# Gated attention over 2048 tokens on one core: sums of tokens resident in SBUF in place of a ring, loads and stores at other places of each unit

## The chip, the cores and the metric

The kernel runs on one core of a Trainium2 chip. The core has five engines, each with its own list of instructions that it works off in order: PE (matrix products), DVE (vector work), ACT (activations and copies), POOL (vector work, slower) and SP, which here only issues transfers between HBM and SBUF. The engines wait for one another by semaphores. The metric is the device time of one execution in microseconds (us); lower is better. Three runs of the kernel before took 2256.18, 2256.52 and 2259.43 us, a median of 2256.52. The profiled execution, from which every view of the trace comes, took 2265.28 us, with a span of 2263.50 on the core.

## The reference

```python
x = A_x                                   # 1 x 2048 x 640
xn = _layernorm(x, axis=-1)
q = (xn @ wq) -> 32 heads of 128
k, v = the last 512 keys of the cache, per head
scores = einsum("bhqd,bhkd->bhqk", q, k) * 128 ** -0.5
o = einsum("bhqk,bhkd->bhqd", softmax(scores), v)
s = o (all heads side by side: 4096) @ wo # 2048 x 640
h = relu(xn @ w1 + b1) ** 2               # 1728 wide
g = silu(h @ w2 + b2)
return x + s * g
```

Everything is float32.

## The kernel before, in words

**Products.** A float32 product is made of three matmuls on pairs: each operand is split into a high and a low part (`hi`, `lo`; ACT copies the high part, POOL or DVE subtracts it from the whole), and high by high, high by low and low by high are summed in PSUM. One such triple on a 128 x 128 weight and 512 tokens is three matmuls (`triple`).

**Tiling.** The tokens are four tiles of 512 (`NT`). The kernel starts with the layer norm, most of the gate (the MLP) and its spill to HBM; then come 128 *units*, one for each pair of a head and a tile. Units 0 to 63 (the first half) do tiles 0 and 3, units 64 to 127 tiles 1 and 2. Four units are a group (`UPG`): two heads by two tiles. At the end follow the rest of the MLP for tile 3 (`late_load`, `late_prep`, `late_up`: raw weights `l1r` and `l2r`, split ones `l1w` and `l2w`, products `lu` and `ly`) and the finish, which multiplies the attention sum `acc` by g (`fg`, loaded by `load_finish`) on DVE and adds x (`fx`) on POOL or DVE.

**One unit i.** PE makes the scores (`s_mm`, four PSUM banks, 12 matmuls). DVE reduces them to column maxima (`max_fold`), ACT gathers these, DVE folds them to a row (`row(i, "m")`, tile `rowm`), and SP writes the 2 KB row to HBM (`m_d`) and reads it back broadcast over the 128 partitions (`bm`, 256 KB). DVE subtracts it from the scores (`shift`, tile `e`), which frees the four score banks: the scores of unit i+1 wait for that. ACT takes exponentials (`expo`) and the high part (`p_hi`), POOL the low part (`p_lo`, tiles `pt`) and the sum of the two halves of the exponentials (`s_add`, tile `su`). DVE folds that sum (`s_fold`, tile `rds`), then `row(i, "s")` makes reciprocals, SP writes them (`s_d`) and reads them back broadcast (`bs`). During the next unit PE multiplies by the values (`v_mm`, bank `o`), DVE scales by `bs` (`o_norm`), ACT and DVE split (`ot`), and after every second unit of a tile PE applies wo (`r_mm`) and DVE adds to `acc` (`r_acc`). So in each unit two small round trips through HBM stand on SP's queue, among the loads of raw keys, values and weights (`kr`, `vr`, `or`, `qr`).

**The queries.** In the first half q comes from five triples per unit. In the second half, two heads by two tiles are done with seven products in place of eight on four of the five chunks: for this the first half makes sums of blocks of wq (`q_sums`, `q_sum_hi`, `q_sum_lo`, tiles `sw`, `ss`) and stores them split in HBM (`q_store`, `wq_d`), and the second half loads them back (`q_piece`, tile `qp`, 512 or 640 KB, one in each unit). The sums of tokens t1 to t4, each of two chunks, lie in HBM (`TS_d`). Part of them is loaded once into `XT`; six pieces of 512 KB that have no room there come anew in every group through a ring of three buffers (`q_ring`, `tr_t`: five pieces; `tr_rest`: two transfers of 256 KB for the last chunk of tile 2).

**What sets the order.** All unit work is put on a list with a time, `at(when, f, ...)`, where a unit has `PERIOD` 12.4; the list is sorted by that time and then emitted, and each engine keeps that order. The numbers are places in an order, not times on the chip. A load is thus issued by SP when SP has come to its place and its buffer is free; whatever stands behind it on SP waits too. BEHIND is a second list: transfers that `row` issues between the write and the broadcast read.

**Where code lies.** The scores of each unit start at a set place of PE's instruction memory: `align` pads to it.

```python
BLOCK, FIRST_SLOT, SLOTS = 256, 188, (0, 11, 22, 33, 42)
pe.addr_align(BLOCK, (FIRST_SLOT + BLOCK // 2 * i + slot) % BLOCK)
```

A unit has 128 slots; its first part with the scores ends at slot 42, and each other matmul takes two with its weight load, so that 54 matmuls in all fit before the next unit's first slot. A unit with more is padded up to that slot one block further on.

**Engines' shares.** Over the span PE is busy 90%, DVE 73%, POOL 60% and ACT 56%.

## Time and profile before

| What | Value |
|---|---|
| median of three runs | 2256.52 us (2256.18 to 2259.43) |
| the profiled execution | 2265.28 us |
| its span | 2263.50 us |
| mean granted clock of PE | 0.961 |
| busy PE / DVE / POOL / ACT | 2032.1 / 1662.1 / 1358.7 / 1257.9 us |
| start of unit 0 / 10 / 59 / 72 / 124 | 298.82 / 433.70 / 1124.30 / 1317.21 / 2063.92 us |
| moved over HBM | 368.69 MB, 163 GB/s |

The stretches between these starts are what the prediction's first view shows. In the views, a row of waits names the engine and its instruction, then what it waited for, the total, the number of times and the longest. A row of the timeline gives start, length, engine, operation and tiles, and in square brackets the idle time of the engine ahead of it with what ended it; `x4` is four instructions shown as one row. SPq is SP's issue of a transfer: its length is that of the issue, not of the transfer. Row names put out before in: `e<-s,bm` writes e and reads s and bm. All instructions have the line of one helper (L77), so tiles tell them apart.

### The profile page before, as it was taken

Reading aid. Unit: us, or ns where it says so; the run is one execution under the profiler, and the core shown is the slowest. Engines: PE = TensorE matmul, PEld = TensorE weight load, DVE = VectorE, ACT = ScalarE, POOL = GpSimd, SP = SyncE. Lnnn points to the kernel's source line nnn. Section 1 sums busy time; section 2 is a strip of 40 time slices with the busy share of each in tenths; the row PEclk is TensorE's granted clock in tenths of the full one; section 3 lists DMA queues with packets and bytes.
Section 4 is the critical chain, followed back from the end, with each engine's and each line's share of the span. In section 5 each row is a group of like instructions: output and inputs, shape, how many; then the busy total and the mean of one; then the engine's idle time right before and its main releaser. Section 6 shows DMA issues by size and latency. Waiting matters only on the chain. (4 is left out here: it accounts for less than half of the span.)

```text
span 2263.5 us, 29971 instructions
## 1 busy us (share of the span) xinstructions
PE 2032.1 (90%) x8489; PEld 1623.0 (72%) x8489; DVE 1662.1 (73%) x2856; ACT 1257.9 (56%) x2232; POOL 1358.7 (60%) x772
## 2 busy tenths in 40 slices
PE   9999999999999999999998888888889888988677
PEld 7887877777777777777776677666677677776566
DVE  6864557788888888888877677777777777777543
ACT  5664446655656555555555555555555555555322
POOL 1031057777777777777776566666666666667431
PEclk9999999999999999999999999999999999999888
DMA  6588744444344344434366555565555455556264
GB/s 196 173 292 293 277 149 138 133 124 122 122 121 122 122 122 122 122 122 122 121 214 205 180 171 169 177 182 179 174 167 169 167 160 165 167 166 190 69 189 143
DMA packets 214385, 368.69 MB, mean 163 GB/s; under 512 B 30084, under 2 KB 89238, under 8 KB 212950
## 3 DMA queue, kind: packets, MB, share of 16 engines
q1 hardware_dynamic: 210358, 350.63, 49.7%
q0 software_dynamic: 3728, 15.99, 1.8%
q8 instruction: 78, 1.28, 0.2%
q14 instruction: 77, 0.63, 0.1%
q10 hardware_dynamic: 144, 0.16, 0.0%
HBM read 293.81 MB, written 72.89 MB: 162 GB/s over the span
## 5 line engine op out<-in xcount | busy, mean ns | idle before, releaser
L77 POOL TENSOR_TENSOR pt<-e,pt 128x1024 fp32r<-128x1024 f32 x256 | 614.2, 2399 | 342.1 <-ACT pt L77 318.9
L77 PE MATMUL s<-q,wk 128*128 128x512 f32 x1536 | 423.9, 430 | 160.2 <-DVE e L77 144.9
L77 PE MATMUL r<-ot,wo 128*128 128x512 f32 x1920 | 494.6, 391 | 5.6 <-DVE acc L77 3.2
L77 PEld LDWEIGHTS s<-q,wk 128*128 128x128 f32 x1536 | 313.7, 208 | 257.7 <-issue 105.5
L77 ACT ACTIVATE e<-e 128x1024 f32<-128x1024 f32 x256 | 269.3, 1052 | 361.4 <-DVE e L77 345.0
L77 PEld LDWEIGHTS r<-ot,wo 128*128 128x128 f32 x1920 | 362.5, 189 | 85.0 <-DVE acc L77 5.2
L77 PE MATMUL o<-pt,wv 128*128 128x512 f32 x1536 | 389.9, 399 | 30.8 <-DVE ot L77 27.8
L77 PEld LDWEIGHTS o<-pt,wv 128*128 128x128 f32 x1536 | 285.6, 190 | 117.1 <-DVE ot L77 40.1
L77 DVE TENSOR_TENSOR e<-s,bm 128x512 f32<-128x512 f32 x512 | 315.9, 676 | 62.5 <-DMA bm<-m_d 62.0
L77 DVE TRANSPOSE_TENSOR_REDUCE rdm<-s 128x16 f32<-128x512 f32 x512 | 328.6, 686 | 38.7 <-PE s L77 38.0
L77 POOL TENSOR_TENSOR su<-e,e 128x1024 f32<-128x1024 f32 x128 | 308.1, 2407 | 0.0
L77 ACT ACTIVATE pt<-e 128x1024 fp32r<-128x1024 f32 x256 | 271.7, 1061 | 7.0
L77 PE MATMUL pq<-ax,wq 128*128 128x512 f32 x960 | 228.2, 389 | 0.0
L77 DVE TENSOR_TENSOR acc<-r,acc 128x512 f32<-128x512 f32 x300 | 200.3, 668 | 10.1 <-PE r L77 9.8
L77 PEld LDWEIGHTS pq<-ax,wq 128*128 128x128 f32 x960 | 180.2, 188 | 37.7
L77 ACT ACTIVATE rdm<-rdm 32x64 f32<-32x64 f32 x384 | 97.8, 255 | 158.7 <-DVE rdm L77 155.7
L77 DVE TRANSPOSE_TENSOR_REDUCE rds<-su 128x32 f32<-128x1024 f32 x128 | 158.3, 1237 | 2.1 <-POOL su L77 2.0
L77 POOL TENSOR_TENSOR wo<-or,wo 128x640 fp32r<-128x640 f32 x64 | 107.3, 1676 | 81.8 <-ACT wo L77 81.8
L77 ACT ACTIVATE rds<-rds 32x32 f32<-32x32 f32 x384 | 90.0, 234 | 115.3 <-DVE rds L77 111.1
L77 DVE TENSOR_TENSOR ot<-o,ot 128x512 fp32r<-128x512 f32 x128 | 88.5, 691 | 77.1 <-ACT ot L77 75.8
L77 ACT ACTIVATE ot<-o 128x512 fp32r<-128x512 f32 x128 | 76.5, 598 | 105.2 <-DVE o L77 105.1
L77 DVE TENSOR_TENSOR o<-o,bs 128x512 f32<-128x512 f32 x128 | 87.5, 684 | 63.9 <-DMA bs<-s_d 63.9
(484 smaller groups left out, 2543.4 us busy)
## 6 DMA issues: line engine op xcount, KB each, us to landing
tr_t<-ts_d SPq DMA_DIRECT2D x80, 512.0 KB
bm<-m_d SPq DMA_DIRECT2D x128, 256.0 KB
bs<-s_d SPq DMA_DIRECT2D x128, 256.0 KB
or<-in_wo_dram SPq DMA_DIRECT2D x64, 320.0 KB
qp<-wq_d SPq DMA_DIRECT2D x32, 640.0 KB
kr<-in_kT_dram SPq DMA_DIRECT2D x64, 256.0 KB
vr<-in_v_dram SPq DMA_DIRECT2D x64, 256.0 KB
wq_d<-ss SPq DMA_DIRECT2D x64, 256.0 KB
```

The costliest lines, as they stand in the source:

```text
L77: ins = method(*args, **kwargs)
```

## The change

- **The ring is gone.** Its six sums get homes in two resident tiles, `ta` and `tb` (`T_HOME`, `open_t`, `load_t`). Three are loaded in the first half, three around the turn of the halves, once. The chunk of `XT` that held a sum now holds the last chunk of tile 2, so that the rest needs no ring either.
- **Room for it.** `s_add` writes over the first half of the exponentials, without `su`. `bm` and the fold tiles have one buffer in place of two. The raw values share the raw keys' buffer, g shares x's; the order of the early finish loads is s, g, x.
- **Stores of `wq_d`** stood at one place of a unit, behind `bs` (11.9). They now stand at two, behind `bm` (4.4, `BM`) and behind `bs` (11.9, `BS`).
- **Loads of `XT` for the second half** went in lots ahead of or behind the broadcast reads in three units for each tile. They now come two transfers of 256 KB at a place, over `BM` and `BS` of units 59 to 64, and BEHIND is gone.
- **The end.** Late in the program the tiles of the sums are closed and a pool `fin` opens, where x and g have two buffers. The wo products of the last but one pair of units have places of their own (`R_AT_LAST`), one of them moved from unit 126 to unit 127. Of the late loads, `LOAD[2]` stands one place later and the first `load_late_x` one place earlier, behind `bm`.

SP's list has 1248 rows where it had 1354. PE, ACT, POOL and DVE have as many instructions of work as before, and in ACT's and POOL's order nothing moves.

SP in the second half, before: from the end of one unit through the next. The numbers in the names are counters; `tr_t` are pieces of the ring.

```order
L77 DMA bs_16816<-s_d_16814 128x512
L77 DMA or_19_16828<-in_wo_dram 128x640
L77 DMA kr_19_16830<-in_kT_dram 128x512
L77 DMA tr_t_16832<-ts_d_81 128x1024
L77 DMA m_d_16906<-rowm_16904 32x16
L77 DMA bm_16908<-m_d_16906 128x512
L77 DMA qp_2_16912<-wq_d_2_121 128x1280
L77 DMA tr_t_16932<-ts_d_81 128x1024
L77 DMA tr_t_16934<-ts_d_82 128x1024
L77 DMA s_d_16961<-rows_16957 16x32
L77 DMA bs_16963<-s_d_16961 128x512
L77 DMA vr_18_16976<-in_v_dram 128x512
```

The same stretch now:

```order
L77 DMA bs_16608<-s_d_16606 128x512
L77 DMA or_19_16620<-in_wo_dram 128x640
L77 DMA kr_19_16622<-in_kT_dram 128x512
L77 DMA m_d_16695<-rowm_16693 32x16
L77 DMA bm_16697<-m_d_16695 128x512
L77 DMA qp_2_16701<-wq_d_2_121 128x1280
L77 DMA s_d_16746<-rows_16742 16x32
L77 DMA bs_16748<-s_d_16746 128x512
L77 DMA vr_18_16761<-in_v_dram 128x512
```

Only the three `tr_t` are gone: one ahead of the write of the maxima, two between the broadcast read `bm` and the write of the sums `s_d`.

SP in the first half, the stores of the block sums, before:

```order
L77 DMA vr_24_9691<-in_v_dram 128x512
L77 DMA or_24_9693<-in_wo_dram 128x640
L77 DMA wq_d_0_131<-wq_9381 256x1x256
L77 DMA wq_d_1_132<-wq_9381 256x1x384
L77 DMA m_d_9763<-rowm_9761 32x16
L77 DMA bm_9765<-m_d_9763 128x512
```

and now, one group earlier in the program:

```order
L77 DMA vr_22_9094<-in_v_dram 128x512
L77 DMA or_22_9096<-in_wo_dram 128x640
L77 DMA m_d_9163<-rowm_9161 32x16
L77 DMA bm_9165<-m_d_9163 128x512
L77 DMA wq_d_0_127<-wq_8785 256x1x256
L77 DMA wq_d_3_130<-wq_8927 256x1x128
L77 DMA wq_d_0_127<-ss_9051 256x1x256
L77 DMA s_d_9218<-rows_9214 16x32
```

The stores moved from ahead of the write `m_d` to behind the broadcast read `bm`, ahead of `s_d`.

PE in unit 126, between its `lu` and the scores of unit 127, before, with the first of the twelve `o` that stand between `r_1` and `r_2`:

```order
L77 MATMUL r_1_20664<-ot_20362,wo_28_0_19845 128x512 x2
L77 MATMUL r_1_20664<-ot_20362,wo_28_1_19846 128x512
L77 MATMUL r_1_20664<-ot_20505,wo_29_0_19702 128x512 x2
L77 MATMUL r_1_20664<-ot_20505,wo_29_1_19703 128x512
L77 MATMUL o_20688<-pt_0_0_20593,wv_31_0_20535 128x512
```

and now the same place, and then the piece of r that follows the scores of unit 127 (`ISA` ends an aligned part):

```order
L77 MATMUL r_1_20346<-ot_20045,wo_28_0_19541 128x512 x2
L77 MATMUL r_1_20346<-ot_20045,wo_28_1_19542 128x512
L77 MATMUL o_20366<-pt_0_0_20274,wv_31_0_20218 128x512
```

```order
L77 MATMUL s_3_20421<-q_0_20204,wk_31_1_19943 128x512
L77 ISA
L77 MATMUL r_1_20346<-ot_20188,wo_29_0_19402 128x512 x2
L77 MATMUL r_1_20346<-ot_20188,wo_29_1_19403 128x512
```

Three matmuls of r went from unit 126, which held 57, to unit 127, behind its scores.

The core of the diff:

```diff
             src = TS_d[0][:, c - NQ2, i, :] if c in (2, 3) else xT_d[T1][i][:, c, :]
         elif c == DC - 1:
-            src = TS_d[3][:, 1, i, :]
+            src = xT_d[T2][i][:, c, :]
         else:
...
     def raw_tile(kind, name):
+        if "fin" in pools and kind in "vsxgw":
+            n = D if kind == "w" else W
+            return pools["fin"].tile(
+                [P, n], F32, tag=f"fin{kind}", name=name, bufs=1 if kind in "vw" else 2
+            )
         n = D if kind in "qo" else W
-        pool_of = pools["ep"] if kind in "qk" else ap
+        pool_of = pools["ep"] if kind in "qkv" else ap
+        kind = {"v": "k", "g": "x"}.get(kind, kind)
         return pool_of.tile([P, n], F32, tag=f"raw{kind}", name=name, bufs=2 if kind == "q" else 1)
 
     def pair(tag, shape, name, bufs):
...
-    def q_ring(n, what):
-        r = QR[n, what] = pools["tr"].tile(
-            [P, 2, NT], F32R, tag="tr", name=f"tr{n}_{what}", bufs=3
-        )
-        if what == "rest":
-            for i in range(2):
-                sp.dma_start(raw(r)[:, i, :], xT_d[T2][i][:, DC - 1, :])
-        else:
-            sp.dma_start(raw(r), TS_d[int(what[1]) - 1][:, int(what[2])])
+    def open_t(n):
+        QR[n] = pools["tr" + n].tile([P, 3, 2, NT], F32R, tag="t" + n, name="t" + n, bufs=1)
+
+    T_HOME = {"t20": "a0", "t21": "a1", "t30": "a2", "t31": "b0", "t40": "b1", "t41": "b2"}
+
+    def load_t(what):
+        n, j = T_HOME[what]
+        sp.dma_start(raw(QR[n])[:, int(j)], TS_d[int(what[1]) - 1][:, int(what[2])])
...
-        for args in BEHIND.pop((i, what), ()):
-            load_x2(*args)
-        bc = ap.tile([P, NT], F32, tag=f"b{what}", name=f"b{what}{i}", bufs=2 if what == "m" else 1)
+        bc = ap.tile([P, NT], F32, tag=f"b{what}", name=f"b{what}{i}", bufs=1)
...
     def s_add(i):
-        RD[i, "su"] = ap.tile([P, 2, NT], F32, tag="su", name=f"su{i}", bufs=1)
-        pool.tensor_tensor(RD[i, "su"], E[i, 0], E[i, 1], op=ALU.add)
+        RD[i, "su"] = E[i, 0]
+        pool.tensor_tensor(E[i, 0], E[i, 0], E[i, 1], op=ALU.add)
...
     def turn_over():
-        pre.close()
-        pools["tr"] = ctx.enter_context(tc.tile_pool(name="tr", bufs=1))
-
+        trb.close()
+        pools["trb"] = trb.enter_context(tc.tile_pool(name="trb", bufs=1))
+        open_t("b")
+
+    def turn_end():
+        trb.close()
+        tra.close()
+        pools["fin"] = ctx.enter_context(tc.tile_pool(name="fin", bufs=1))
+
+    BM, BS = 4.4, 11.9
...
+        for k, lo, what, *places in (
+            (0, 2, (0, 0, 2), (0, BM), (0, BM), (-2, BM)),
+            (3, 0, (0, 4, 5), (0, BM), (-1, BM), (-2, BM)),
+            (1, 0, (0, 2, 5), (0, BS), (-1, BM), (-2, BM)),
+            (2, 0, (1, 2, 5), (1, BM), (1, BM), (-1, BM)),
+            (3, 1, (1, 4, 5), (1, BM), (0, BM), (-1, BM)),
+            (0, 0, "s1", (2, BM), (0, BM), (0, BM)),
+            (1, 3, "s2", (2, BM), (1, BM), (0, BM)),
+            (2, 3, "s3", (2, BS), (2, BM), (1, BM)),
+            (3, 2, "s4", (2, BS), (2, BS), (1, BM)),
         ):
-            pre_at(u, 4.4 if end and u == 1 else 11.9, q_store, k, lo, what)
-    at((NU // 2 - 3) * PERIOD + 10.0, turn_over)
-
+            u, when = places[0 if first else 2 if end else 1]
+            pre_at(u, when, q_store, k, lo, what)
...
+    b = NU // 2
+    at((b - 24) * PERIOD, open_t, "a")
+    at((b - 3) * PERIOD + 8.0, turn_over)
...
+    for u, when, pieces in (
+        (-22, BM, ("t20",)),
+        (-18, BM, ("t21",)),
+        (-14, BM, ("t30",)),
+        (-5, BM, ((0, 2),)),
+        (-5, BS, ((0, 3),)),
+        (-4, BM, ((0, 0),)),
+        (-4, BS, ((0, 1),)),
+        (-3, BS, ((1, 0), (0, 4))),
+        (-2, BM, ((1, 1),)),
+        (-2, BS, ("t31",)),
+        (-1, BM, ("t40",)),
+        (-1, BS, ("t41",)),
+        (0, BM, ((1, 2),)),
+        (0, BS, ((1, 3), (1, 4))),
+    ):
+        for what in pieces:
+            if isinstance(what, str):
+                at((b + u) * PERIOD + when + 0.05, load_t, what)
+            else:
+                for i in range(2):
+                    at((b + u) * PERIOD + when + 0.05, load_x2, what[0], i, what[1])
...
+    R_AT_LAST = (
+        ((3 * PERIOD + 2.75, range(G)),),
+        ((3 * PERIOD + 7.75, range(1)), (4 * PERIOD + 2.75, range(1, G))),
+        ((3 * PERIOD + 11.25, range(G)),),
+        ((4 * PERIOD + 7.0, range(G)),),
+        ((4 * PERIOD + 7.6, range(G)),),
+    )
+    R_BANK_LAST = ("x", "x", 0, "x", 0)
...
-            if slot == 0:
-                on(4.45, q_ring, n, "t20")
-                on(4.45, q_ring, n, "t21")
-                on(10.4, q_ring, n, "t30")
-            elif slot == 1:
-                on(7.6, q_ring, n, "t31")
-                on(7.6, q_ring, n, "t40")
-            elif slot == 2:
-                on(4.45, q_ring, n, "rest")
...
-        2: z - 2 * PERIOD + 10.3,
+        2: z - PERIOD + 4.5,
...
-        at(z - 3 * PERIOD + (10.3, 16.8, 16.85, 22.7, 22.75)[c], load_late_x, c)
+        at(z - 3 * PERIOD + (4.5, 16.8, 16.85, 22.7, 22.75)[c], load_late_x, c)
+    at(z - 3 * PERIOD + 9.2, turn_end)
```

More of the change, by code (lines that the diff above doesn't have):

```diff
@@ L858, in bank @@
         return pools["psa"].tile([P, NT], F32, tag=f"qr{k}", name=name, bufs=1)
-    BEHIND = {}
     def open_xT(hf, t):
@@ L997, in q_right @@
     def q_right(n, what, q):
-        if (n, f"{what}{q}") in QR:
-            r = QR[n, f"{what}{q}"]
-            return r[:, 0, :], r[:, 1, :]
-        t, c = (1, 3) if what == "t4" else RES[what]
+        if f"{what}{q}" in T_HOME:
+            k, j = T_HOME[f"{what}{q}"]
+            return [QR[k][:, int(j), i, :] for i in range(2)]
+        t, c = RES[what]
         return [x[:, c + q, :] for x in XT[1, t]]
@@ L1017, in q_rest @@
         w = QP[n, k]
-        if t == 0:
-            xs = [x[:, DC - 1, :] for x in XT[1, 0]]
-        else:
-            r = QR[n, "rest"]
-            xs = r[:, 0, :], r[:, 1, :]
+        xs = [x[:, DC - 1, :] for x in XT[1, t]]
         triple(
@@ L1071, in fold_tile @@
         n = KC if what == "m" else 2
-        return ap.tile([P, NQ, P // B32, n], F32, tag=f"rd{what}", name=f"rd{what}{i}", bufs=2)
+        return ap.tile([P, NQ, P // B32, n], F32, tag=f"rd{what}", name=f"rd{what}{i}", bufs=1)
     def max_fold(i, c):
@@ L1233, in late_load @@
         else:
-            tag, bufs = ("su", 1) if kind == 1 else ("e", 2)
-            r = ap.tile([P, 2, NT], F32, tag=tag, name=f"l{kind}r{f}", bufs=bufs)
-            r = r.rearrange("p a b -> p (a b)")[:, :D]
+            if kind == 1:
+                r = raw_tile("w", f"l{kind}r{f}")
+            else:
+                r = ap.tile([P, 2, NT], F32, tag="e", name=f"l{kind}r{f}", bufs=2)
+                r = r.rearrange("p a b -> p (a b)")[:, :D]
         if kind == 1:
@@ L1323, in late_relu @@
         ph = LPH[f]
-        r = LR[f] = raw_tile(kind, f"lr{f}")[:n, :]
+        if kind == "s":
+            r = pools["tra"].tile([P, 3, 2, NT], F32, tag="ta", name=f"lr{f}", bufs=1)[:, 0, 0]
+        else:
+            r = raw_tile(kind, f"lr{f}")
+        r = LR[f] = r[:n, :]
         bias = b1_sb[:n, f : f + 1]
@@ L1395, in late_gate @@
         tag = ("bm", "bs")[(d + lo * 2 // NT) % 2]
-        sg = ap.tile([P, NT], F32, tag=tag, name=f"lsg{d}_{lo}", bufs=2 if tag == "bm" else 1)[:, : hi - lo]
+        sg = ap.tile([P, NT], F32, tag=tag, name=f"lsg{d}_{lo}", bufs=1)[:, : hi - lo]
         act.activation(sg, LPY[py], AF.Silu, bias=b2_sb[:, d : d + 1])
@@ L1552 @@
     at(10.0, pad, pools["ep"], 480)
-    pools["pre"] = pre = ExitStack()
-    pools["pre"] = pre.enter_context(tc.tile_pool(name="pre", bufs=1))
+    tra, trb = ExitStack(), ExitStack()
+    pools["tra"] = tra.enter_context(tc.tile_pool(name="tra", bufs=1))
+    pools["pre"] = trb.enter_context(tc.tile_pool(name="pre", bufs=1))
     def turn_over():
-        pre.close()
-        pools["tr"] = ctx.enter_context(tc.tile_pool(name="tr", bufs=1))
+        trb.close()
+        pools["trb"] = trb.enter_context(tc.tile_pool(name="trb", bufs=1))
+        open_t("b")
@@ L1560 @@
+    def turn_end():
[3 more added lines that the diff above has]
+    BM, BS = 4.4, 11.9
     for n in range(NG):
         base = UPG * PERIOD * n
-        end = n == NG - 1
+        first, end = n == 0, n == NG - 1
         def pre_at(u, when, f, *a):
-            at(max(base + u * PERIOD, 0.0) + when if n else max(u, 0) * PERIOD + when, f, n, *a)
-        pre_at(-2, 9.5, q_sums, 0)
-        pre_at(-1, 5.0 if end else 9.5, q_sums, 1)
+            assert n or u >= 0
+            at(base + u * PERIOD + when, f, n, *a)
+        pre_at(0 if first else -2, 9.5, q_sums, 0)
+        pre_at(0 if first else -1, 5.0 if end else 9.5, q_sums, 1)
@@ L1569 @@
         for k in range(4):
-            u = k // 2 - 1 if end else k - 1
-            if n == 0:
-                u = 1 + k // 2
+            u = 1 + k // 2 if first else k // 2 - 1 if end else k - 1
             pre_at(u, 7.0 + 0.01 * k, q_sum_hi, k)
             pre_at(u, 9.0 + 0.01 * k, q_sum_lo, k)
-        late = n == 0
-        for u, k, lo, what in (
-            (-1 + late, 0, 2, (0, 0, 2)),
-            (-1 + late, 1, 0, (0, 2, 5)),
-            (0 + late, 2, 0, (1, 2, 5)),
-            (0, 3, 0, (0, 4, 5)),
-            (0, 3, 1, (1, 4, 5)),
-            (0 if end else 1, 0, 0, "s1"),
-            (0 if end else 1, 1, 3, "s2"),
-            (1 if end else 2, 2, 3, "s3"),
-            (1 if end else 2, 3, 2, "s4"),
-        ):
-            pre_at(u, 4.4 if end and u == 1 else 11.9, q_store, k, lo, what)
@@ L1588 @@
-    at((NU // 2 - 3) * PERIOD + 10.0, turn_over)
-    for t in range(TPH):
-        u = NG * UPG + t * G - 5
-        at(u * PERIOD + 4.3, open_xT, 1, t)
-        pieces = [
-            (t, i, c) for c in ((2, 3, 0, 1, 4), (0, 1, 2, 3, 4))[t] for i in range(2)
-        ]
-        places = [(u, "bm", 1 - t), (u - 1, "s", 2 - t), (u + 1, "m", 1), (u + 1, "bm", 1)]
-        places += [(u, "s", 2), (u + 2, "m", 1), (u + 2, "bm", 1 + t), (u + 1, "s", 1 + t)]
-        for k, what, n in places:
-            for args in pieces[:n]:
-                if what == "bm":
-                    at(k * PERIOD + 4.3, load_x2, *args)
-                else:
-                    BEHIND.setdefault((k, what), []).append(args)
-            pieces = pieces[n:]
-        assert not pieces
+        for k, lo, what, *places in (
[8 more added lines that the diff above has]
+            (3, 2, "s4", (2, BS), (2, BS), (1, BM)),
+        ):
+            u, when = places[0 if first else 2 if end else 1]
+            pre_at(u, when, q_store, k, lo, what)
@@ new lines @@
+    b = NU // 2
+    at((b - 24) * PERIOD, open_t, "a")
+    at((b - 3) * PERIOD + 8.0, turn_over)
+    for t in range(TPH):
+        at((b - 5 + t * G) * PERIOD + 4.3, open_xT, 1, t)
+    for u, when, pieces in (
[17 more added lines that the diff above has]
+                at((b + u) * PERIOD + when + 0.05, load_t, what)
+            else:
+                for i in range(2):
+                    at((b + u) * PERIOD + when + 0.05, load_x2, what[0], i, what[1])
@@ L1718 @@
                         k = k[d]
+                    elif i == NU - 2 * G - 1:
+                        places, k = R_AT_LAST, R_BANK_LAST[d]
                     else:
                         places, k = R_AT_Q[t], "x"
+                        if d == 0 and i == NQS - 1:
+                            places = (
+                                ((2 * PERIOD + 11.25, range(1)), (3 * PERIOD + 2.75, range(1, G))),
+                            )
                     for when, js in places[d]:
@@ L1726 @@
                     w = (NU // 2 + 9 + 4 * d) * PERIOD
-                    for k, n in enumerate("sxg" if t == 0 else ""):
-                        at(w + k * PERIOD - 0.6, load_finish, n, 0, t, d)
                     if t == 0:
-                        at(w + 3 * PERIOD - 0.7, finish_gate, 0, t, d)
+                        for k, n in enumerate("sgx"):
+                            at(w + k * PERIOD - 0.6, load_finish, n, 0, t, d)
+                        at(w + 2 * PERIOD - 0.7, finish_gate, 0, t, d)
                         at(w + 3 * PERIOD - 0.7, finish, 0, t, d)
```

## The prediction

> **What bounds the kernel now.** I read the busy time by stage first. The cuts lie where units 10, 59, 72 and 124 start; the columns are the stretch, its length, then busy time and count of PE, PEld, DVE, ACT and POOL, the granted clock, the DMA share and GB/s.

> ```profile
> 433.70:1124.30 690.60, 632.58 (x2648) 505.31 (x2646) 560.20 (x956) 407.12 (x735) 526.77 (x296) 0.97 0.41 122
> 1124.30:1317.21 192.91, 166.02 (x681) 130.16 (x682) 137.95 (x238) 109.28 (x197) 123.43 (x63) 0.97 0.60 196
> 1317.21:2063.92 746.71, 660.71 (x2730) 522.75 (x2731) 577.38 (x994) 418.18 (x741) 488.21 (x239) 0.97 0.55 170
> 2063.92:2263.50 199.58, 154.97 (x617) 122.67 (x617) 98.53 (x151) 71.12 (x117) 74.52 (x43) 0.88 0.45 143
> ```

> No engine is full anywhere. The third stretch is 13 groups of four units, 57.44 us each, with PE busy 50.8 of it (matmuls at the slower clock included) and DVE 44.4. Next the waits of that stretch (us in total, times, longest):

> ```profile
> DVE o L77 <- DMA bs<-s_d: 40.6, 26, 2.8
> DVE e L77 <- DMA bm<-m_d: 35.3, 27, 3.1
> ```

> 26 and 27 times in 13 groups: two units of each four have DVE stand for both broadcasts, 75.9 us or 5.84 a group. PE's timeline of one group shows which units:

> ```profile
> 1751.01 2.88 PE L77 MATMUL s<-q,wk 128*128 128x512 f32 x12
> 1763.41 2.88 PE L77 MATMUL s<-q,wk 128*128 128x512 f32 x12
> 1779.98 2.97 PE L77 MATMUL s<-q,wk 128*128 128x512 f32 x12 [3.50 <-DVE e L77]
> 1794.76 2.98 PE L77 MATMUL s<-q,wk 128*128 128x512 f32 x12 [1.56 <-DVE e L77]
> 1807.45 2.88 PE L77 MATMUL s<-q,wk 128*128 128x512 f32 x12
> ```

> The units 102 to 105 take 12.40, 16.57, 14.78 and 12.69 us, 56.44 together. The two long ones end in PE waiting for e, the shift that frees the score banks. SP's issues around them say why, and two rows of the page's issue list give the sizes:

> ```profile
> 1761.86 0.32 SPq L77 DMA_DIRECT2D s_d<-rows  x1
> 1766.87 0.32 SPq L77 DMA_DIRECT2D bs<-s_d  x1
> ...
> 1768.84 0.33 SPq L77 DMA_DIRECT2D m_d<-rowm  x1
> 1774.21 0.32 SPq L77 DMA_DIRECT2D bm<-m_d  x1
> 1774.62 0.38 SPq L77 DMA_DIRECT2D qp<-wq_d  x1
> 1775.06 0.90 SPq L77 DMA_DIRECT2D tr_t<-ts_d  x2
> 1776.60 0.32 SPq L77 DMA_DIRECT2D s_d<-rows  x1
> 1783.38 0.32 SPq L77 DMA_DIRECT2D bs<-s_d  x1
> ```

> ```profile
> 1800.12 0.32 SPq L77 DMA_DIRECT2D m_d<-rowm  x1
> 1801.44 0.32 SPq L77 DMA_DIRECT2D bm<-m_d  x1
> 1801.85 0.54 SPq L77 DMA_DIRECT2D qp<-wq_d  x1
> 1806.28 0.32 SPq L77 DMA_DIRECT2D s_d<-rows  x1
> 1807.61 0.33 SPq L77 DMA_DIRECT2D bs<-s_d  x1
> ```

> ```profile
> tr_t<-ts_d SPq DMA_DIRECT2D x80, 512.0 KB
> qp<-wq_d SPq DMA_DIRECT2D x32, 640.0 KB
> ```

> The write of 2 KB and the broadcast read behind it take 1.33 us of SP where qp was issued 4.43 us before and nothing else, and 5.01 and 6.78 us where ring pieces were issued before; for the maxima 1.32 against 5.37. So the tuned bound is a queue: small round trips behind ring pieces.

> **Part A, the ring goes (units 72 to 123).** The PE, ACT, POOL and DVE instructions stay the same in number (8489 matmuls before and now). SP loses 80 ring pieces and 32 rests. Each was an issue of about 0.45 us (0.90 for two at 1775.06) on an engine that bounds nothing, so the issues count as nought; what counts is the queue. I follow the two long units on DVE and POOL:

> ```profile
> 1771.31 0.70 DVE L77 TENSOR_TENSOR o<-o,bs 128x512 f32<-128x512 f32 x1 [1.90 <-DMA bs<-s_d]
> 1773.28 1.24 DVE L77 TRANSPOSE_TENSOR_REDUCE rds<-su 128x32 f32<-128x1024 f32 x1
> 1779.14 2.48 DVE L77 TENSOR_TENSOR e<-s,bm 128x512 f32<-128x512 f32 x4 [1.99 <-DMA bm<-m_d]
> 1785.15 2.41 POOL L77 TENSOR_TENSOR su<-e,e 128x1024 f32<-128x1024 f32 x1
> 1787.48 0.70 DVE L77 TENSOR_TENSOR o<-o,bs 128x512 f32<-128x512 f32 x1 [2.18 <-DMA bs<-s_d]
> 1789.45 1.24 DVE L77 TRANSPOSE_TENSOR_REDUCE rds<-su 128x32 f32<-128x1024 f32 x1
> 1793.94 2.47 DVE L77 TENSOR_TENSOR e<-s,bm 128x512 f32<-128x512 f32 x4
> ```

> Unit 103: with a 1.3 us round trip o starts at 1771.31 - 1.90 = 1769.41, rds at 1773.28 - 1.90 = 1771.38. DVE was ready for e at 1779.14 - 1.99 = 1777.15, 3.87 after rds began, so now 1775.25. bm would be issued at 1768.84 + 1.32 = 1770.16 and, landing as slowly as now (1774.21 to 1779.14, 4.93), is there at 1775.09, in time. PE's s follows e's first piece by 0.84 (1779.98 - 1779.14): 1776.09, so 12.68 us in place of 16.57.

> Unit 104: o could start at 1787.48 - 2.18 = 1785.30. What is late next is su on POOL, which ends at 1785.15 + 2.41 = 1787.56; rds starts there and not at 1789.45, 1.89 sooner. e comes as much sooner (1792.05), s 0.82 behind it at 1792.87: 12.89 in place of 14.78. The group is 12.40 + 12.68 + 12.89 + 12.69 = 50.66, 5.78 less; over 13 groups 75. The 5.84 us of DMA waits a group, from the other view, agree. The mean group is 1.00 longer than this one, by pauses of the same kind; I take 0.8 of it away as well, 10 more. **A = 85**; bounds: half of the waits stay, 38, and the whole difference between 57.44 and four units of 12.40, 102.

> [...]

> The new resident tiles add six loads of 512 KB, once. Summing in place costs the same POOL instruction (2.41); its buffer of e is now free only after rds, but rds stands ahead of the next unit's e on DVE anyway: nought, and a wait of 1.24 at the most (rds itself) if that order did not hold. With one buffer, bm of a unit must wait for e of the unit before, which ended before that unit's own s could run: nought.

> **Part B, loads at the turn (units 59 to 71).** 13 units take 192.91 us. At A's pace they would take 13 x 50.66 / 4 = 164.6; so the gain lies between 0 and 28. The 5 MB of x and sums must still come in there, at the highest DMA share of the rows above (0.60), only in smaller lots. I take three fifths: **B = 17**.

> **Part C, the tail.** Waits of PE from 2063.92 on, and rows of the timeline:

> ```profile
> PE s L77 <- issue: 15.2, 1, 15.2
> PE lu L77 <- POOL l1w L77: 14.1, 3, 7.7
> PE lu L77 <- DMA ax<-xT_d: 2.4, 1, 2.4
> ```

> ```profile
> 2102.07 3.14 PE L77 MATMUL lu<-ax,l1w 128*128 128x512 f32 x6 [2.42 <-DMA ax<-xT_d]
> 2126.35 4.66 PE L77 MATMUL s<-q,wk 128*128 128x512 f32 x12 [15.24 <-issue]
> 2188.16 0.69 DVE L77 TENSOR_TENSOR acc<-acc,fg 128x512 f32<-128x512 f32 x1 [5.48 <-DMA fg<-g_d]
> ```

> The pause of 15.24 has no releaser in the trace. Unit 126 holds 57 matmuls ahead of the aligned s of unit 127, and the blocks of 128 slots have room for 54; I read the pause as PE's sequencer stepping through padding to the next block. With r placed so that 54 stand there it goes (15.2), and s behind it runs in 2.88 and not 4.66 (1.8). The first ax is issued one place earlier, ahead of the large loads: 2.4, and six lu at 3.14 that would run in half of that (1.6). The l1w waits come down a chain: fg has one buffer, the gating waits for fg (5.48), POOL's add for that, and POOL's split of l1w stands behind the add; with two buffers for x and g the loads are a step ahead: 14.1. **C = 35**; bounds: 17 if the pause is something else and a third of the l1w waits stays, 45 if the slow matmuls behind each of these pauses recover too.

> [...]

> **Part D, the first half (units 10 to 58).** The stores of wq_d move from one place behind bs to two. DVE's wait there is

> ```profile
> DVE e L77 <- DMA bm<-m_d: 12.1, 12, 1.4
> ```

> once a group. Without a store ahead of m_d it goes; stores now lie between bm and s_d, up to 640 KB. Where only qp lay between, SP had 4.84 us from bm to s_d (1801.44 to 1806.28), and the queue moved qp, two ring pieces and bm, 1.9 MB, in the 9.2 us from 1774.21 to 1783.38, some 0.2 MB a us: 640 KB are through in 3.1 us, ahead of s_d. Stores that SP reaches before their split is done would hold s_d: the loss of such a hold is no larger than the wait taken away. **D = 12**, bounds -5 and 25 (the wait doubles up with the pause behind it).

> **The sum.** 85 + 17 + 35 + 12 = 149. The profiled execution took 2265.28 us (span 2263.50 and 1.78 around it), so 2116.3; the runs' median of 2256.52 is 8.76 below the profiled time, so **2107.5 us**, 6.6% less.

> **The rivals.** *Half of A stays.* qp, kr, vr and or still share the queue. Moving everything earlier by 3.9 us in unit 103 brings s_d nearer to qp, and su or PE's own work may take over: 210 matmuls a group (2730 / 13) at the 12.40 / 54 us of unit 102, which pauses nowhere, are 48.2 us. For it: a group of 50.66 leaves PE 2.4 us of pause in four units, and no four units show that yet. Against: units 102 and 105 run at 12.40 and 12.69 with the same qp behind bm. A group near 54 gives 3.6 x 13 = 47 for A and 9 for B: 149 - 38 - 8 = 103, **2153 us**.

> *The pause in the tail stays.* The trace names no releaser. If PE's pause is a fetch of code or else and not padding, 17 come back: **2124 us**.

> *Slower.* The value and the key rows now share one staging buffer, so SP, which issues in order, stands at each kr or vr until POOL has split the tile before. If that split were over 5 us into the next unit, the write of the maxima behind it would be late in every unit, as in unit 103. At 3.5 us of pause for each of the 49 units from 433.70 to 1124.30 that is 171 against A + B + C = 137: 2256.5 + 34 = **2291 us**; it decides from 2.8 us a unit. Against it: POOL is busy 526.77 of 690.60 us there and the split comes ahead of the next s.

> **How the numbers follow.** The forecast 0.64, half of A 0.22, the tail's pause 0.10, slower 0.03, no change (all three terms given back by one new wait) 0.01. The likeliest is 2107.5. Its bounds (A 38 to 102, B 0 to 28, C 17 to 45, D -5 to 25) do not fall together; the first rival's 2153 with some of D lost gives 2165, and upwards half of the spare 17 + 11 + 10 + 13 gives about 2080. So 2080 to 2165. A measurement of this kernel tells some 0.2% from no change; faster by more than that 0.95, within it 0.02, slower 0.03.

> **What would show it.** Right: DVE's waits for bs and bm in units 72 to 123 fall from 75.9 us to under 15 and the groups to 51; PE's issue pause in front of the last s is gone; lu waits for l1w under 3 us. Wrong: SP's distance from s_d to bs stays over 3 us in two units of four, or s waits for e as long as now with another name behind e (su, rds). A new wait of SP ahead of m_d would show as DVE's e waiting for bm in every unit of the first half, and would make the forecast wrong in sign.

## The result and the profile after

The changed kernel takes 2128.09 us (2127.05 to 2130.55, four runs) against 2257.32 us of the kernel before beside it (2256.18 to 2259.43): a ratio of 0.9428, 95% interval 0.9412 to 0.9444. The forecast was 2107.5 us in a range of 2080 to 2165. The profiled execution took 2127.05 us, its span is 2125.20.

Busy time by stage of the changed kernel, cut where units 10, 59, 72 and 124 start, with the columns of the prediction's first view:

```profile
432.49:1109.11 676.62, 622.17 (x2648) 499.92 (x2646) 560.49 (x955) 406.75 (x735) 528.62 (x296) 0.98 0.41 128
1109.11:1287.76 178.65, 163.43 (x681) 128.43 (x682) 140.16 (x238) 109.07 (x197) 122.97 (x62) 0.98 0.54 170
1287.76:1952.29 664.53, 632.82 (x2732) 506.78 (x2731) 570.28 (x994) 417.15 (x741) 491.72 (x241) 1.00 0.42 130
1952.29:2125.20 172.91, 149.66 (x617) 119.32 (x617) 103.92 (x151) 70.61 (x117) 77.03 (x44) 0.94 0.49 158
```

| Stage | before | after | difference | forecast |
|---|---|---|---|---|
| up to unit 10 | 433.70 | 432.49 | -1.2 | 0 |
| units 10 to 58 (D) | 690.60 | 676.62 | -14.0 | -12 |
| units 59 to 71 (B) | 192.91 | 178.65 | -14.3 | -17 |
| units 72 to 123 (A) | 746.71 | 664.53 | -82.2 | -85 |
| from unit 124 on (C) | 199.58 | 172.91 | -26.7 | -35 |
| span | 2263.50 | 2125.20 | -138.3 | -149 |

In the third stage a group of four units now takes 51.12 us (664.53 / 13; before 57.44), PE's clock is 1.00 where it was 0.97, and the DMA share 0.42 where it was 0.55. The waits of that stage (us, times, longest) which answer to those shown before:

```profile
PE s L77 <- DVE e L77: 30.6, 26, 2.1
DVE e L77 <- DMA bm<-m_d: 5.8, 10, 0.9
```

The first of these rows read before:

```profile
PE s L77 <- DVE e L77: 65.2, 28, 4.6
```

DVE's wait for bs, 40.6 us before, has no row any more; that for bm fell from 35.3 to 5.8 us, and PE's wait for e from 65.2 to 30.6. SP's issues in two units of one group show the queue without the ring:

```profile
1693.30 0.34 SPq L77 DMA_DIRECT2D bm<-m_d  x1
1693.69 0.43 SPq L77 DMA_DIRECT2D qp<-wq_d  x1
1697.72 0.32 SPq L77 DMA_DIRECT2D s_d<-rows  x1
1699.04 0.32 SPq L77 DMA_DIRECT2D bs<-s_d  x1
...
1704.36 0.33 SPq L77 DMA_DIRECT2D m_d<-rowm  x1
1705.81 0.33 SPq L77 DMA_DIRECT2D bm<-m_d  x1
```

From s_d to bs are 1.32 us where it was 5 to 6.8, from m_d to bm 1.45 where it was 5.37. These are short ones. The means over the 13 groups, for the four units of a group (numbers 0 to 3, the unit's number modulo 4), show that the queue is not empty now:

| SP's distance, us | before | now |
|---|---|---|
| m_d to bm | 2.91, 1.62, 1.48, 5.64 | 2.32, 1.36, 1.46, 1.36 |
| s_d to bs | 1.45, 5.42, 6.86, 4.26 | 1.35, 2.00, 1.55, 2.76 |

In unit 3 of a group, s_d to bs is still over 3 us in 5 of the 13 groups.

The tail is where the forecast was missed most. PE's waits from 1952.29 on:

```profile
PE lu L77 <- POOL l1w L77: 11.3, 3, 5.4
PE ly L77 <- ACT l2w L77: 3.6, 1, 3.6
PE s L77 <- DVE e L77: 2.6, 2, 1.6
PE lu L77 <- DMA ax<-xT_d: 1.7, 2, 1.5
```

Two further rows of PE's waits in the tail before:

```profile
PE s L77 <- DVE e L77: 6.6, 3, 3.5
PE ly L77 <- ACT l2w L77: 5.1, 2, 3.5
```

The scores of unit 127 in the timeline now:

```profile
1995.11 2.88 PE L77 MATMUL s<-q,wk 128*128 128x512 f32 x12
```

The pause of 15.24 us is gone and the scores run in 2.88 us where they took 4.66, but lu still waits 11.3 us for l1w (before 14.1). Rows of the timeline around the first two of these waits:

```profile
2053.53 0.69 DVE L77 TENSOR_TENSOR acc<-acc,fg 128x512 f32<-128x512 f32 x1 [5.53 <-DMA fg<-g_d]
2054.30 1.64 POOL L77 TENSOR_TENSOR acc<-acc,fx 128x512 f32<-128x512 f32 x1 [8.19 <-DVE acc L77]
2055.91 2.11 POOL L77 TENSOR_TENSOR l1w<-l1r,l1w 128x640 fp32r<-128x640 f32 x1
...
2058.60 1.41 DVE L77 TENSOR_TENSOR acc<-acc,fx 128x512 f32<-128x512 f32 x1
...
2060.04 0.34 SPq L77 DMA_DIRECT2D out_dram<-acc  x1
2060.43 0.42 SPq L77 DMA_DIRECT2D fx<-in_xT_dram  x1
2060.95 0.40 SPq L77 DMA_DIRECT2D fg<-g_d  x1
...
2064.88 0.69 DVE L77 TENSOR_TENSOR acc<-acc,fg 128x512 f32<-128x512 f32 x1 [3.66 <-DMA fg<-g_d]
...
2067.28 2.11 POOL L77 TENSOR_TENSOR l1w<-l1r,l1w 128x640 fp32r<-128x640 f32 x1
```

SP issues the loads of x and g only behind the store of a finished piece (2060.04), which waits for the add (DVE's, done at 2060.01). The buffers were not what held them: with two in turn, this g goes into the one that the gating at 2053.53 read last (done at 2054.22), this x into the one that POOL's add freed at 2055.94. From the issue of fg come 3.9 us until g is there, then the gating, POOL's add, and only then POOL's split of l1w.

### The profile page after: what moved, and what is told of

It reads as the page before. It is cut to its first block, busy times and chain, and to the rows that moved or that the text cites. A ratio compares the mean times of both kernels' runs of the same rounds, so it can differ in the third digit from the quotient of the medians.

```text
span 2125.2 us, 29624 instructions
## 1 busy us (share of the span) xinstructions
PE 1982.8 (93%) x8489; PEld 1594.7 (75%) x8489; DVE 1663.6 (78%) x2856; ACT 1256.7 (59%) x2232; POOL 1367.2 (64%) x772
## 5 line engine op out<-in xcount | busy, mean ns | idle before, releaser
L77 POOL TENSOR_TENSOR pt<-e,pt 128x1024 fp32r<-128x1024 f32 x256 | 615.3, 2403 | 276.5 <-ACT pt L77 269.0
L77 PE MATMUL r<-ot,wo 128*128 128x512 f32 x1920 | 493.8, 390 | 1.8 <-DVE q L77 1.2
L77 PE MATMUL s<-q,wk 128*128 128x512 f32 x1536 | 390.3, 404 | 99.2 <-DVE e L77 99.2
L77 ACT ACTIVATE e<-e 128x1024 f32<-128x1024 f32 x256 | 269.5, 1053 | 311.5 <-DVE e L77 293.8
L77 PEld LDWEIGHTS s<-q,wk 128*128 128x128 f32 x1536 | 292.4, 194 | 185.7 <-DVE e L77 76.7
L77 PEld LDWEIGHTS r<-ot,wo 128*128 128x128 f32 x1920 | 361.0, 188 | 79.9 <-DVE q L77 1.6
L77 PE MATMUL o<-pt,wv 128*128 128x512 f32 x1536 | 382.9, 394 | 6.3 <-POOL pt L77 3.0
L77 PEld LDWEIGHTS o<-pt,wv 128*128 128x128 f32 x1536 | 284.8, 188 | 83.9 <-POOL pt L77 21.6
L77 DVE TRANSPOSE_TENSOR_REDUCE rdm<-s 128x16 f32<-128x512 f32 x512 | 326.8, 685 | 7.0 <-PE s L77 6.4
L77 DVE TENSOR_TENSOR e<-s,bm 128x512 f32<-128x512 f32 x512 | 315.1, 673 | 16.7 <-DMA bm<-m_d 15.9
L77 POOL TENSOR_TENSOR e<-e,e 128x1024 f32<-128x1024 f32 x128 | 308.3, 2408 | 10.0
L77 ACT ACTIVATE pt<-e 128x1024 fp32r<-128x1024 f32 x256 | 271.8, 1062 | 6.9
L77 PE MATMUL pq<-ax,wq 128*128 128x512 f32 x960 | 228.1, 389 | 0.0
L77 PEld LDWEIGHTS pq<-ax,wq 128*128 128x128 f32 x960 | 180.2, 188 | 37.6
L77 DVE TENSOR_TENSOR acc<-r,acc 128x512 f32<-128x512 f32 x300 | 200.1, 667 | 6.5 <-PE r L77 6.4
L77 ACT ACTIVATE rdm<-rdm 32x64 f32<-32x64 f32 x384 | 97.8, 255 | 126.2 <-DVE rdm L77 123.1
L77 DVE TRANSPOSE_TENSOR_REDUCE rds<-e 128x32 f32<-128x1024 f32 x128 | 158.5, 1238 | 3.0 <-POOL e L77 2.1
L77 ACT ACTIVATE rds<-rds 32x32 f32<-32x32 f32 x384 | 89.8, 234 | 108.5 <-DVE rds L77 104.7
L77 DVE TENSOR_TENSOR ot<-o,ot 128x512 fp32r<-128x512 f32 x128 | 88.5, 691 | 82.6 <-ACT ot L77 82.5
L77 POOL TENSOR_TENSOR wo<-or,wo 128x640 fp32r<-128x640 f32 x64 | 107.6, 1681 | 40.8 <-ACT wo L77 40.8
L77 DVE TENSOR_REDUCE rowm<-rdm 32x16 f32<-32x256 f32 x128 | 52.1, 407 | 91.4 <-ACT rdm L77 84.6
L77 POOL TENSOR_TENSOR wv<-vr,wv 128x512 fp32r<-128x512 f32 x64 | 83.7, 1308 | 46.0 <-ACT wv L77 46.0
## 6 DMA issues: line engine op xcount, KB each, us to landing
qp<-wq_d SPq DMA_DIRECT2D x32, 512.0 KB
```

The source lines that it names most:

```text
L77: ins = method(*args, **kwargs)
```

## The experiments

Ratios are to the kernel before, run beside each. Stages are cut at the starts of the same units as above.

**The ring's traffic once more, in pairs.** The resident sums are loaded again into their own places, so that only transfers are added. The slot counts units from two ahead of a group.

```diff
+    AGAIN = {2: ((4.45, "t20"), (4.45, "t21")), 3: ((4.45, "t30"), (4.45, "t31")), 0: ((4.45, "t40"), (4.45, "t41"))}
...
             at(t0 - PERIOD + 4.4, q_piece, n, slot)
+            for when, what in AGAIN.get(slot, ()) if NG < n < HALF * NG - 1 else ():
+                on(when, load_t, what)
```

> The changed kernel, with the six sums loaded again in place in each of 14 groups of the second half, though they are resident: two pieces of 512 KB behind bm in three units of four, 3 MB a group as the ring moved before. Nothing waits for them that did not wait before. If the time was lost because small round trips stood behind large transfers on the queue: SP's distance from s_d to bs grows from 1.4 to 2.8 us to 5 us and more in three units of four, the groups go from 51.1 to 54 to 57 us, the time from 2128 to 2170 to 2210 us. If the ring cost its time by something else (its buffers, PE waiting for a piece, a code place), the time stays at 2128 to 2135 us.

Measured: 2182.7 us (2180.37 to 2185.15), ratio 0.9648 (0.9631 to 0.9665). The stage of units 72 to 123, and DVE's waits in it:

```profile
1299.84:2010.83 710.99, 650.37 (x2731) 509.20 (x2731) 576.09 (x994) 417.34 (x741) 490.25 (x240) 0.99 0.57 177
```

```profile
DVE o L77 <- DMA bs<-s_d: 25.2, 30, 1.8
DVE e L77 <- DMA bm<-m_d: 16.0, 17, 1.9
```

46.5 us more than without these loads, and not because an operand comes later: the trace has no wait of PE for `ta` or `tb`, and SP's waits for PE come to 2.0 us in this stage (3.4 without the loads). So it is the transfers themselves, and not the waiting for the ring's data, that hold the round trips. A group takes 54.7 us, as expected. From s_d to bs the means in the four units of a group are 3.60, 4.99, 2.39 and 5.97 us: three units of four are longer, as expected, though one of them by less than the 5 us that I gave.

**The same traffic, spread.** One piece behind bm and one behind bs, in the same units:

```diff
+    AGAIN = {2: ((4.45, "t20"), (11.95, "t21")), 3: ((4.45, "t30"), (11.95, "t31")), 0: ((4.45, "t40"), (11.95, "t41"))}
```

> The same six loads a group, one at a place: one behind bm and one behind bs in three units of four. If it is the lot behind one small transfer that counts: 640 + 512 KB at some 0.2 MB a us are 5.6 us against 4.8 us from bm to s_d, so s_d to bs stays under 3 us, the groups within 1.5 us of 51.1, the time between 2128 and 2150 us. If it is the bytes a group, it is as slow as with pairs (2170 to 2210 us).

Measured: 2204.48 us (2203.1 to 2208.22), ratio 0.9747 (0.973 to 0.9764). The stage and the waits:

```profile
1303.04:2030.70 727.66, 655.32 (x2730) 516.77 (x2731) 576.46 (x994) 417.23 (x741) 489.69 (x239) 0.98 0.54 173
```

```profile
DVE e L77 <- DMA bm<-m_d: 54.2, 34, 3.9
DVE o L77 <- DMA bs<-s_d: 3.5, 8, 0.9
```

Spreading made it worse, 63.1 us over the stage without the loads. My working, in which a lot of 1.15 MB fits between two round trips and costs nothing, is refuted: s_d to bs takes 3.07, 5.29, 3.21 and 4.20 us on the mean in the four units of a group, not under 3, and m_d to bm 2.38, 2.47, 3.45 and 3.23 (in the changed kernel 2.32, 1.36, 1.46 and 1.36). Now 34 shifts wait for bm, where 17 did with pairs. A piece behind bs stands ahead of the next m_d, and a piece behind bm ahead of s_d; both trips lie on DVE's chain, so that this spreading puts one in front of each of the two. Of these two arrangements of the same bytes the one with fewer places is the better; both are slower than none.

**The same traffic at the ring's very places.**

```diff
+    AGAIN = {
+        0: ((4.45, "t20"), (4.45, "t21"), (10.4, "t30")),
+        1: ((7.6, "t31"), (7.6, "t40")),
+        2: ((4.45, "rest"),),
+    }
```

> The changed kernel with the resident sums loaded again at the very places where the ring's loads stood: two pieces behind bm, one ahead of the next m_d, two behind the next bm, two of 256 KB behind the third. If the traffic and its places are all that the ring cost: units 72 to 123 take 740 to 750 us again (664.5 without, 711.0 with pairs, 727.7 spread), the time is 2203 to 2212 us. If part of the cost was the ring's three buffers (a load that SP can only issue when PE has read an older piece, with the round trips held behind it), the stage stays at 700 to 725 us, and the rest up to 746.7 is the buffers' share.

Measured: 2218.9 us (2215.05 to 2221.38), ratio 0.9814 (0.9792 to 0.9836). The stage and the waits:

```profile
1303.10:2041.84 738.74, 660.73 (x2730) 522.90 (x2731) 577.67 (x994) 418.24 (x741) 489.77 (x239) 0.96 0.54 170
```

```profile
DVE e L77 <- DMA bm<-m_d: 35.4, 26, 2.9
DVE o L77 <- DMA bs<-s_d: 29.1, 21, 2.2
```

74.2 of the 82.2 us of this stage come back, with PE busy as long as before (660.73 against 660.71) and DVE's wait for bm the same to 0.1 us. The loads are in only 12 of the 13 groups, 60 pieces where the ring issued 65; so 6.2 us a group come back of the 6.3 that the ring cost. That leaves next to nothing for the ring's three buffers, and the waits agree: SP's waits for PE come to 5.1 us in this stage of the kernel before, and to 3.4 in the changed kernel, which has no ring. (Two executions of the changed kernel differ by 3 us in this stage, 664.53 and 667.59.) The stage is 1 us short of the expected band, the total 7 us above its own: units 59 to 71, with the loads from unit 66 on, lose 15.1 us too (193.77 against 178.65), which I had not counted. That is as much as the whole gain of part B.

**The stores back at one place.** In the first half, the table of the kernel before:

```diff
-            (0, 2, (0, 0, 2), (0, BM), (0, BM), (-2, BM)),
-            (3, 0, (0, 4, 5), (0, BM), (-1, BM), (-2, BM)),
...
+            pre_at(u, 4.4 if end and u == 1 else 11.9, q_store, k, lo, what)
```

> The changed kernel with the stores of wq_d at the one place of before, all behind bs. If the 14 us of the first half came from them: the first half (units 10 to 58) goes from 676.6 back to 688 to 692 us, DVE waits for bm again once a group, the time is 2139 to 2144 us. If they came from the other edits there (the sums in place, single buffers, fewer pauses by chance), the time stays within 3 us of 2128.

Measured: 2141.21 us (2135.64 to 2144.66), ratio 0.947 (0.945 to 0.949). The stage of units 10 to 58, and a row of DVE's waits in it:

```profile
433.37:1117.66 684.29, 625.43 (x2648) 501.98 (x2646) 559.05 (x956) 407.16 (x735) 529.16 (x296) 0.98 0.40 126
```

```profile
DVE e L77 <- DMA bm<-m_d: 9.5, 12, 1.0
```

In the changed kernel that row was

```profile
DVE e L77 <- DMA bm<-m_d: 0.2, 1, 0.2
```

The wait is back, 12 times as before, and 7.7 of the stage's 14.0 us with it. The stage fell short of the band I gave (688 to 692). Seven executions with the changed kernel's first half took 676.6 to 679.5 us there, so the move of the stores is worth 5 to 8 us, about half of D; which edit brings the rest was not taken apart.

**The tail's three matmuls alone.** The kernel before with this edit only:

```diff
+                    elif i == NU - 2 * G - 1:
+                        places, k = R_AT_LAST, R_BANK_LAST[d]
                     else:
                         places, k = R_AT_Q[t], "x"
```

> The kernel before with one edit: three matmuls of wo moved from unit 126 (57 matmuls, now 54) to unit 127. If the pause of 15.24 us ahead of the last scores is padding up to the next block: it is gone and the scores behind it run in 2.9 and not 4.7 us, 2240 us in place of 2257. If the pause is something else that stands at this point of the program (code that is fetched, a semaphore that the trace does not show), it stays, 2256 to 2258 us.

Measured: 2241.28 us (2239.46 to 2243.62), ratio 0.9907 (0.9891 to 0.9924), beside 2262.59 us: 21 us less. The timeline of PE at the end of unit 126:

```profile
2102.64 1.52 PE L77 MATMUL r<-ot,wo 128*128 128x512 f32 x6
2104.00 2.88 PE L77 MATMUL s<-q,wk 128*128 128x512 f32 x12
```

No pause, and the scores run in 2.88 us where they took 4.66. The stage from unit 124 on takes 182.16 us where it took 199.58, 17.4 less; the other 4 us of the 21 lie in other stages and are no more than two executions of one kernel differ by. That the pause is padding the trace shows too: between the scores of units 126 and 127 PE's sequencer works off 268 NOPs in the kernel before, at most 37 between any other two, and 36 here. In the pause of 15.24 us lie 205 of them, as a rule 0.071 us apart and nowhere over 0.25, which leaves no room for a wait for code.

**One buffer for the last x and g.**

```diff
-                [P, n], F32, tag=f"fin{kind}", name=name, bufs=1 if kind in "vw" else 2
+                [P, n], F32, tag=f"fin{kind}", name=name, bufs=1
```

> The changed kernel with one buffer in place of two for x and g of the last finish. If the two buffers gave the 2.8 us by which lu's waits for l1w fell (14.1 to 11.3): those waits are 13 to 16 us, the time 2130 to 2134 us. If they gave nothing, because SP issues a pair's loads only behind the store of the pair before in any case: 2127 to 2130 us.

Measured: 2133.92 us (2130.89 to 2133.99), ratio 0.9436 (0.9417 to 0.9456). PE's wait in its tail, and the tail:

```profile
PE lu L77 <- POOL l1w L77: 14.3, 3, 7.2
```

```profile
1954.42:2132.00 177.58, 150.86 (x617) 120.49 (x617) 97.97 (x151) 70.87 (x117) 76.24 (x44) 0.92 0.48 154
```

The wait is 3.0 us longer than with two buffers and as long as in the kernel before; the ratio cannot be told from the changed kernel's. The tail as a whole is 4.7 us longer than the changed kernel's 172.91, and seven executions with the changed kernel's tail took 170.5 to 172.9 us. So the two buffers gave 3 us of this wait and 5 to 7 us in all.

**The last loads ahead of the stores.**

```diff
-                [P, n], F32, tag=f"fin{kind}", name=name, bufs=1 if kind in "vw" else 2
+                [P, n], F32, tag=f"fin{kind}", name=name, bufs=1 if kind in "vw" else 4
...
-                at(z + 30.0 + 6.5 * t + 8.0 * d, load_finish, n, HALF - 1, t, d)
+                at(z + 22.0 + 6.5 * t + 8.0 * d, load_finish, n, HALF - 1, t, d)
```

> The changed kernel with four buffers for x and g of the last finish, and their loads placed 8.0 earlier, so that they stand ahead of the stores that wait for POOL and DVE. If lu waits for l1w because fg arrives late behind SP's stores: DVE's waits for fg go, lu's waits for l1w fall from 11.3 to under 3 us, the slow matmuls behind them recover some 4 us, and the time is 2112 to 2118 us. If POOL is late for another reason (l1r's own load, ACT's copy), the waits stay at 9 us or more, 2126 to 2130 us.

Measured: 2110.91 us (2108.91 to 2112.66), ratio 0.9337 (0.9317 to 0.9357). The tail:

```profile
1958.09:2107.20 149.11, 140.24 (x617) 113.20 (x617) 104.42 (x151) 70.78 (x117) 78.13 (x44) 1.00 0.58 183
```

All that PE still waits for there:

```profile
PE s L77 <- DVE e L77: 2.4, 2, 1.6
PE ly L77 <- ACT l2w L77: 1.7, 1, 1.7
PE lu L77 <- DMA ax<-xT_d: 0.7, 2, 0.5
```

172.91 us have become 149.11, lu has no wait for l1w left, DVE's wait for fg (22.5 us in the changed kernel's tail) has no row any more, and the clock of this stage is 1.00 in place of 0.94. So l1w was late because fg was, and fg because its load stood behind SP's stores, as the timeline above showed. How much the earlier places would give with two buffers in place of four was not run.

**The sums of wq behind the shift.** DVE's largest wait left in the first half, PE's wait for e there, and one case of it in the changed kernel's timeline:

```profile
DVE sw L77 <- POOL ss L77: 44.7, 13, 3.4
PE s L77 <- DVE e L77: 52.4, 25, 2.8
```

```profile
666.62 0.43 DVE L77 TENSOR_TENSOR sw<-qr 128x256 f32<-128x256 f32 x1 [3.44 <-POOL ss L77]
...
668.16 4.46 PE L77 MATMUL s<-q,wk 128*128 128x512 f32 x12 [2.77 <-DVE e L77]
```

```diff
-        pre_at(0 if first else -2, 9.5, q_sums, 0)
-        pre_at(0 if first else -1, 5.0 if end else 9.5, q_sums, 1)
+        pre_at(0 if first else -2, 9.5 if first else 11.85, q_sums, 0)
+        pre_at(0 if first else -1, 5.0 if end else 9.5 if first else 11.85, q_sums, 1)
```

> The changed kernel with one more edit in the first half: DVE's sums of wq blocks (sw, which wait 3.4 us for POOL's split ss in one unit of four) stand behind the shift of the scores in DVE's order, not ahead of it. If that wait is what PE's pause of 2.8 us ahead of the scores comes from: the pause and the half-rate scores behind it go (2.8 + 1.6 us a group), the sums of the next unit give 0.5 more; 14 groups, 2060 to 2075 us. If another wait takes its place (POOL, the raw weights, max_fold behind the sums), 2110 us or more.

Measured: 2080.64 us (2079.16 to 2081.31), ratio 0.9205 (0.9183 to 0.9226). The stage of units 10 to 58, and the wait in it:

```profile
430.72:1061.54 630.82, 618.27 (x2648) 490.44 (x2646) 547.70 (x956) 406.05 (x736) 529.63 (x295) 1.00 0.44 137
```

```profile
DVE sw L77 <- POOL ss L77: 6.8, 10, 1.1
```

PE's wait of s for e has no row any more in this stage. It takes 45.8 us less; the expected 2.8 + 1.6 + 0.5 us a group would be 60 us in these 49 units, and the time is 6 us above the band. By their place in the group the units took 12.8, 12.2, 15.2 and 14.9 us on the mean, and now 13.1, 12.8, 12.2 and 13.4: the two long ones give up 4.5 us, the two others take 0.9 back.

**Both.** The two edits together:

> The changed kernel with both edits: the sums of wq blocks behind the shift, and the last loads of x and g ahead of the stores with four buffers. They lie in different stages (units 0 to 59, and the tail), so their gains should add: the ratios to the kernel before were 0.9428 for the changed kernel, 0.9205 and 0.9337 with one edit each, so 0.911 with both, 2056 to 2064 us. If one wait only moves into the other's stage, 2070 us or more.

Measured: 2063.27 us (2061.11 to 2069.01), ratio 0.9128 (0.9111 to 0.9146). The gains add: the sum of the single ones, 0.911, lies at the lower end of the interval. This is the fastest version here, 8.7% below the kernel before.

**The changed kernel again.**

> The changed kernel once more, beside the others and on another chip than the first time. The kernel before scattered over 2255.9 to 2266.1 us here, the changed one over 2127.1 to 2130.6 on its chip. If the scatter comes from pauses that sometimes bring PE's slower clock, the changed kernel, which has fewer pauses of over 2.4 us, scatters less (within 6 us); the ratio stays within 0.940 to 0.946.

Measured: 2133.37 us (2128.37 to 2134.19), ratio 0.9426 (0.9411 to 0.9441), beside 2262.51 us (2256.36 to 2264.25). The ratio holds; the times of both kernels lie some 5 us higher than in the first comparison. The changed kernel scattered over 5.8 us in five runs and the kernel before over 7.9 in nine, so that fewer pauses making for less scatter is suggested and not shown.

## Why the prediction was right, and where it was off

- **What bounds the kernel: right.** The waits for bs and bm were the cost of the second half, and they came from transfers on the queue: the same loads without any need for them bring 74.2 us back.
- **A, 85 us: 82.2 measured.** The step that followed two units on DVE and POOL gave a group of 50.66 us; the groups take 51.12. PE still waits 30.6 us for e, in 26 of 52 units, and the round trips behind qp are not as short as I took them (up to 2.76 us on the mean against 1.3).
- **B, 17 us: 14.3 measured,** half of the room of 28 and not three fifths; the share was a guess, and that it came near is in part luck. The ring's loads alone, put back from unit 66 on, take back 15.1 us here (9.2 in pairs, 14.4 spread) with the loads of x at their new places. So B is the ring once more, and no run shows a gain from the smaller lots. The sum counted 5 MB of loads here; SP issues 6.7 MB of x and sums, where it issued 13.8 with the ring's 8.7.
- **D, 12 us: 14.0 measured,** of which the stores' move carries 5 to 8. The wait for bm went as reckoned (12.1 to 0.2 us), but it is only about half of the gain; that the size fits is in part luck.
- **C, 35 us: 26.7 measured. This is the term that was mis-sized, by one step:** "with two buffers for x and g the loads are a step ahead: 14.1". I took the buffer to be what held the load. It was SP's order: each pair's loads stand behind a store that waits for the add of an earlier pair. Of the 14.1 us came 2.8, and 11.3 stayed where I had named under 3 as the sign of being right; with the loads ahead of the stores and four buffers the wait was gone. The row of ax was also too hopeful: two waits of 1.7 us in all are left of 2.4, with slow matmuls behind them (five lu in 1.97 us at 1986.92, where ten took 2.46 at 2013.47). The pause of 15.24 us went as reckoned, 17.4 us with what hung on it against 17.0. So of the other 18 us of C came 9.3, and of these the sum had not listed the scores' wait for e, 6.6 us before and 2.6 now.
- **From the profile to the median: wrong.** I took the 8.76 us by which the profiled execution stood above the median for a fixed distance and carried them over. The kernel before scatters from 2255.91 to 2266.14 us over all its runs here, its profile was near the upper end of that, and the changed kernel's profiled execution (2127.05) stood 1.04 us below its median. Of the 20.6 us by which the forecast was too low, 9.8 come from this and 10.8 from the terms.
- **The rivals.** Half of A staying is refuted by the groups of 51.12 us. That the pause in the tail is no padding is refuted by the edit alone. The slower case, SP held at the shared buffer of raw keys and values, did not come: in units 10 to 58 SP waits 16.0 us in all for POOL's splits of keys and values (before, it did not wait for them), never over 1.0 us at a time, where 2.8 us in every unit would have been needed; and DVE's wait for bm there is 0.2 us. No run gave the values a buffer of their own again, so a small cost of the sharing stays open.

## What to carry to other kernels

Look at what the queue holds ahead of a small round trip through HBM that an engine waits for: here s_d to bs took 1.33 us of SP with only qp 4.43 us before, and 5.01 and 6.78 us behind ring pieces. What helped was to move fewer bytes there (82.2 us in units 72 to 123), while the same bytes spread over more places stood in front of both trips, and the stage took 727.66 us where it took 710.99 in pairs. Before giving a late load a second buffer, look at what SP must issue ahead of it: here a store that waited for an add (2060.04) held the loads of x and g behind it, though their buffers had been free since 2055.94 and 2054.22; their loads at earlier places, with four buffers, brought the tail from 172.91 to 149.11 us. When a sum of stage gains from one profiled execution is turned into a median, look at the scatter of the runs first: the distance between one execution and the median did not carry over here (8.76 us above it before, 1.04 us below it now).

## What the runs showed of the hardware that was not expected

PE's slower clock did not set in at one length of pause here. Over the twelve profiled executions (the two kernels and the ten runs) I sorted the 1536 groups of twelve score matmuls by the pause ahead of them, and counted as slow those whose twelve starts were spread over more than 3.2 us (2.5 to 2.7 in groups that ran at full clock):

| pause ahead, us | groups | slow |
|---|---|---|
| under 1.6 | 1212 | 0 |
| 1.6 to 2.0 | 84 | 4 |
| 2.0 to 2.4 | 20 | 10 |
| 2.4 to 2.8 | 117 | 64 |
| 2.8 to 3.2 | 22 | 14 |
| 3.2 to 3.6 | 49 | 41 |
| over 3.6 | 32 | 32 |

A pause of under 1.6 us ahead of the scores never made them slow in these traces (0 of 1212), one of 2.4 to 2.8 us did about every second time (64 of 117) and one of over 3.6 us each time (32 of 32), and a slow group cost some 1.6 us beside the pause (4.46 against 2.88).

The records of the granted clock in the same traces show what it went with beside the length. In each trace every change of the clock lies on a grid of 3.41 us (in those of the two kernels to within 0.003 us), and the half rate (0.5 in the records) lasts whole steps of it: in the two kernels' traces one to four, but for the last record, which ends with the trace. From unit 0 on, 6208 steps ran at full clock:

| PE busy in the step | steps | half rate in the next |
|---|---|---|
| under 42% | 196 | 196 |
| 42 to 60% | 264 | 33 |
| 60% and more | 5748 | 0 |
